# Holding seven in-place weight differences in program order, inside block 2's first product

## The chip, the cores and the metric

The kernel runs on one core of a Trainium2 chip. The metric is device time in microseconds, from one launch that has the inputs in the chip's memory to the finished output there; lower is better. A profiled execution also gives a span, which runs from the first to the last instruction, and is a little shorter than the device time.

The core has engines that run side by side, each with a queue of its own that is worked off in order: TensorE (PE in the profile; PEld is its weight load), VectorE (DVE), ScalarE (ACT), GpSimd (POOL) and SyncE (SP), which here only issues transfers. SBUF is the working memory of 128 partitions, PSUM the memory into which TensorE writes its sums.

## The reference

A retention layer, step by step in time, and then a feed-forward block with a sigmoid-gated activation:

```
B, H, S, D = 4, 8, 768, 64            # q, k, v
state = zeros(B, H, D, D)
for t in range(S):
    state = gamma[h] * state + outer(k[t], v[t])
    y[t]  = (q[t] @ state) / sqrt(D)
x = y as (B*S, H*D) = (3072, 512)
h = x @ w_in                          # 512 x 2048
g = h * sigmoid(1.702 * h)
out = g @ w_out                       # 2048 x 512 -> (3072, 512), float32
```

## The kernel before, in words

The 3072 tokens are worked off in six blocks (`m` = 0 to 5). For each block the first product makes h = x · w_in with the activation behind it, and the second makes g · w_out. The steps of the retention for the next block (L287 to L310 on TensorE, with transposes L251, masks L316 and outputs L345 on VectorE) are strewn between the pieces of a second product.

**Products with fewer multiplications.** The 2 x 2 scheme with seven products instead of eight (Strassen's in Winograd's form) is used for blocks of matrices. It needs sums and differences of quarters of both operands. `sums_w1`, `sums_w2`, `sums_x` (L437 to L441, on POOL) and `sums_g` (L452 to L456) make these. After them `W2` holds seven 128-partition slots of w_out's sums, each of 8 x 256 values per partition.

From block 2 on the second product is cut twice (`down49`, seven times seven products): each of the seven slots of `W2` is itself split into four quarters b11, b12, b21, b22, and three inner sums t1, t2, t4 and one difference t3 of these are wanted. They don't all fit in SBUF. `inner_w2(i)` makes three of them in a scratch part of `X` with three chained VectorE subtractions (L520) and stores them to memory (`W2D`, L521; the first four stores are issued by SP, the last three by POOL). Each call has to wait until the store of the call before has landed, since all use the same scratch. The calls stand at seven places of blocks 0 and 1, the list `INNER`; the last three are in block 1, behind its pieces 12, 15 and 18. Later a ring in SBUF is filled from `W2D` again (`stream`, L543).

**The seven differences of the title.** The fourth inner value, t3 = b22 - b12, replaces b12 in place: `inner_w2_t3(i)`, one VectorE subtraction of 128 x 512 values on line 527, called for i = 0 to 6. It needs b12 in its old state no more: the call of `inner_w2(i)` has read it, and block 1, which uses the slots of W2 uncut, must have done its products with that slot. In the program these calls stand in the loop over the rounds d = 0 to 3 of block 2's first product `up(d)`, two behind each of the first three rounds and one behind the last.

**A round of the first product** (`up`, L463 to L505) has seven matrix products of TensorE, 8 matmul instructions each, in the order x, y1, x, y2, x, y3, x. The four to `x` add up in one PSUM tile, and between them ScalarE copies what has been summed (p1 on L477, u on L484, vv on L491). VectorE adds these copies to y1, y2 and y3 (L480, L488, L494, L496), ScalarE applies the activation (L391, within `hidden`), and VectorE ends the round with four differences of the result (L502 to L505). TensorE can't add to x before the copy of it has been read. The copies p1 and t share one buffer (tag s1), and so does the `t` of block 1's second product. Behind round 0 come the two transposes L251 of a retention step.

**The end of block 1.** `down(1)` has 28 pieces. Its last additions to the output (L683) are made on VectorE into `o`, which has two buffers, and each is stored by a transfer that POOL issues (L684). Four POOL subtractions prepare the activations (L460), POOL makes the decayed keys (L272), and then `sums_x` on POOL prepares X for block 2 (L438 to L441).

**What sets the order.** TensorE's queue has the order of the program. The other queues are ordered ahead of time by a planner, which works with estimates of its own for the time of each instruction: of the instructions that could go next it takes an early one, and may draw an instruction ahead of others that stand before it in the program. `tc.keep_in_program_order(...)` binds an instruction behind the one that was written before it on the same engine, as an order only and not as a wait for its end. L520, L521, L251, L316, L345, L454 to L456, L460 and L684 are held so. L480, L505, L683, L272 and L438 to L441 aren't, and nor is L527.

Of the kernel before, what the change touches and what calls it, by code (L numbers as in the profile page):

```python
# [28 lines left out]
def kernel(  # L29
# [29 lines left out]
    pe, act, dve, pool, sp = nc.tensor, nc.scalar, nc.vector, nc.gpsimd, nc.sync  # L59
# [450 lines left out]
    def w2q(w):  # L510

        return [W2[:, w, u::2, e * P:(e + 1) * P] for u in range(2) for e in range(2)]
# [11 lines left out]
    def inner_w2_t3(i):  # L524

        b11, b12, b21, b22 = w2q(ORDER[i][1])
        dve.tensor_sub(b12, b22, b12)  # L527

    def sums_g_outer(k):

# [334 lines left out]
    for m in range(NB):  # L865
# [13 lines left out]
        if m > 1:  # L879
            if m > 2:  # L880
                W1B[:] = [late.tile([P, 2, 7, 2, P], F32, name=f"W1B{i}", tag=f"late{i}") for i in range(2)]
                pool.dma_start(W1B[0], W1D[0])
            for d in range(NP // 2):
                up(d)
                if d == 0 and m > 2:
                    pool.dma_start(W1B[1], W1D[1])
                if d == 0 and m < NB - 1:
                    turn((m + 1) * CB + 1)
                if d == NP // 2 - 2:
                    ring = begin_ring()  # L890
                if m == 2 and d < 2:
                    tc.keep_in_program_order(sp.dma_start(W1D[d], W1B[d]))
                if m == 2:
                    for i in range(2 * d, min(7, 2 * d + 2)):
                        inner_w2_t3(i)
# [62 lines left out]
```

## Time and profile before

| | |
|---|---|
| median of 6 runs | 673.8 us |
| lowest and highest | 671.99 and 676.49 us |
| the profiled execution | 671.99 us |
| its span | 670.3 us |
| granted clock of TensorE | 0.996 |
| block 1's last pieces end, block 2's first product begins | 267.16 us |
| block 2's second product begins | 319.64 us |

Times within the profile are microseconds from the start of the span. In the timeline each line has the start, the duration (for several instructions in one line, of all of them), the engine, the line of the code, the operation and its tiles, output before the arrow and inputs behind it. A bracket tells how long the engine was idle before and what ended the idle time. In the list of waits a line gives the waiting engine and line, what it waited for, the total, the count and the longest.

### The profile page before, as it was taken

What the parts mean: (1) busy time and instruction counts of PE and PEld (TensorE: products, weight loads), DVE (VectorE), ACT (ScalarE), POOL (GpSimd) and SP (SyncE); (2) the same over time, 40 slices, a digit from 0 to 9 for tenths busy, and PEclk for the clock granted to TensorE, in tenths of its full rate; (3) what the DMA queues carried; (4) which work ended last, traced back from release to release, by engine and by line L of the source; (5) the groups of instructions that cost most, each with busy time, mean ns of one, the idle gap of its engine ahead of it and who ended that gap; (6) DMA issues with size and microseconds to landing.
All of it is one profiled execution on the core that took longest, in us unless ns stands there. A gap on an engine that the chain in (4) does not pass through costs nothing.

```text
span 670.3 us, 15330 instructions
## 1 busy us (share of the span) xinstructions
PE 653.1 (97%) x6502; PEld 567.0 (85%) x6502; DVE 439.3 (66%) x614; ACT 156.9 (23%) x313; POOL 171.6 (26%) x192
## 2 busy tenths in 40 slices
PE   6899999999999999799999999999999999999997
PEld 4788864747888888688999988999988999988997
DVE  4798880879845879454986264996264995254965
ACT  5675523321000000233110233110233110233110
POOL 3000000020278325200345700254800255400000
PEclk9899999999999999999999999999999999999999
DMA  9999742332303546354286652277662243602142
GB/s 184 220 218 232 190 126 80 133 89 46 71 13 130 166 107 162 87 169 177 68 197 161 195 154 95 65 175 175 171 190 94 64 145 111 249 2 95 50 156 96
DMA packets 143781, 88.98 MB, mean 133 GB/s; under 512 B 129472, under 2 KB 130752, under 8 KB 142688
## 3 DMA queue, kind: packets, MB, share of 16 engines
q1 hardware_dynamic: 134224, 45.97, 30.4%
q0 software_dynamic: 7184, 40.78, 16.9%
q10 hardware_dynamic: 2304, 1.25, 0.6%
q8 instruction: 51, 0.84, 0.5%
q14 instruction: 18, 0.15, 0.1%
HBM read 72.37 MB, written 15.47 MB: 131 GB/s over the span
## 4 chain that ended last, share of the span: by engine, by line
PE 90%; DMA 3%; DVE 2%; SPq 2%; POOL 1%; issue 1%; ACT 0%; POOLq 0%; ACTq 0%; DVEq 0%
PE pq L574 26%; PE px L470 16%; PE py L470 12%; PE pd L707 10%; PE ph L412 8%; PE ph L425 8%; PE pt L248 2%; PE pa L287 2%; PE py L310 2%; PE pa L295 1%; PE py L304 1%; DMA kn_in<-in_k_dram 1%; DMA q_in<-in_q_dram 1%; SPq L137 1%; DMA W2D<-X 1%
## 5 line engine op out<-in xcount | busy, mean ns | idle before, releaser
L574 PE MATMUL pq<-W,G 128*128 128x128 f32 x672 | 80.2, 276 | 0.0
L574 PEld LDWEIGHTS pq<-W,G 128*128 128x128 f32 x672 | 77.6, 192 | 0.6
L543 POOL DMA_DIRECT2D ring<-W2D x28 | 15.4, 551 | 230.8 <-PE px L470 120.4
L470 PE MATMUL px<-X,W1A 128*128 128x256 f32 x256 | 60.0, 380 | 3.0 <-ACT p L477 3.0
L470 PE MATMUL px<-X,W1B 128*128 128x256 f32 x256 | 59.8, 379 | 0.0
L574 PE MATMUL pq<-ring,own 128*128 128x128 f32 x448 | 59.8, 276 | 0.0
L470 PEld LDWEIGHTS px<-X,W1A 128*128 128x128 f32 x256 | 48.2, 190 | 9.9 <-issue 3.3
L574 PEld LDWEIGHTS pq<-ring,own 128*128 128x128 f32 x448 | 54.5, 192 | 0.4
L470 PEld LDWEIGHTS px<-X,W1B 128*128 128x128 f32 x256 | 48.6, 190 | 6.6
L707 PE MATMUL pd<-W,G 128*128 128x256 f32 x224 | 49.8, 381 | 0.1
L707 PEld LDWEIGHTS pd<-W,G 128*128 128x128 f32 x224 | 42.1, 190 | 6.3 <-POOL G L460 0.5
L470 PE MATMUL py<-X,W1A 128*128 128x256 f32 x192 | 45.5, 380 | 0.6 <-DVE o L683 0.6
L470 PE MATMUL py<-X,W1B 128*128 128x256 f32 x192 | 45.4, 379 | 0.0
L391 ACT ACTIVATE G<-G 128x512 f32<-128x512 f32 x48 | 30.2, 630 | 51.1 <-DVE G L480 32.4
L470 PEld LDWEIGHTS py<-X,W1A 128*128 128x128 f32 x192 | 36.4, 190 | 5.9 <-DVE o L683 1.0
L470 PEld LDWEIGHTS py<-X,W1B 128*128 128x128 f32 x192 | 36.5, 190 | 5.0
L488 DVE TENSOR_TENSOR t<-py,u 128x512 f32<-128x512 f32 x16 | 11.1, 692 | 35.7 <-PE py L470 35.7
L477 ACT ACTIVATE p<-px 128x512 f32<-128x512 f32 x16 | 9.6, 597 | 100.4 <-PE px L470 87.4
L574 PE MATMUL pq<-ring,G 128*128 128x128 f32 x224 | 29.6, 275 | 0.0
L574 PE MATMUL pq<-W,own 128*128 128x128 f32 x224 | 29.6, 275 | 0.0
L412 PE MATMUL ph<-X,W1A 128*128 128x256 f32 x128 | 29.1, 383 | 0.2 <-DVE X L345 0.2
L502 DVE TENSOR_TENSOR G<-G 128x512 f32<-128x512 f32 (+2 forms) x24 | 12.3, 513 | 25.7 <-ACT G L391 25.7
(203 smaller groups left out, 1181.5 us busy)
## 6 DMA issues: line engine op xcount, KB each, us to landing
ring<-W2D POOLq DMA_DIRECT2D x28, 768.0 KB, 4.9
W1B<-W1D POOLq DMA_DIRECT2D x6, 1792.0 KB, 9.2
W<-in_moe_w_in_dram SPq DMA_DIRECT2D x12, 512.0 KB, 5.2
W<-in_moe_w_out_dram SPq DMA_DIRECT2D x10, 512.0 KB, 3.7
out_dram<-o POOLq DMA_DIRECT2D x20, 256.0 KB, 3.2
v_in<-in_v_dram SPq DMA_DIRECT2D x64, 64.0 KB, 3.2
q_sq<-in_q_dram SPq DMA_DIRECT2D x128, 32.0 KB, 2.2
k_sq<-in_k_dram SPq DMA_DIRECT2D x128, 32.0 KB, 2.2
```

Of the source, the lines that this page charges most:

```text
L248: pe.matmul(p[n][HALF[r], s, :], x[n][:, HP * r + s, :], ident, start=True, stop=True)
L287: pe.matmul(pa[HALF[w], u, 0, s, :], kt[HALF[u], w, s, :], qt[HALF[u], w, s, :], start=True, stop=True)
L310: pe.matmul(py[HALF[o], w, 0, 2 * u + s2 if f < 2 * CB else 2 * s2 + u, :], vn[HALF[w], HP * u + s, :], a[HALF[w], u, s, :], start=True, s ...
L391: pin(act.activation(g, h[:, i], AF.Gelu_apprx_sigmoid))
L412: pe.matmul(h[:, ab], w, X[:, 2 * th + c // 2, c % 2, :], start=(ab == 0 and c == 0), stop=(c == 3), skip_group_check=True)
L425: pe.matmul(h, w, X1[:, c // 2:4:2, c % 2, :], start=(c == 0), stop=(c == 3))
L470: pe.matmul(acc[:, u, :], t[:, q1 + u, sa, c, :], X[:, sb, c, :], start=(start and u == 0 and c == 0), stop=(stop and c == 1), skip_group_ ...
L488: dve.tensor_add(tt, z, u)
L502: dve.tensor_sub(q[0][1], q[0][0], q[0][1])
L543: pool.dma_start(c, W2D[i])
L574: pe.matmul(p0[:, j, :], a[:, d], w[:, d], start=(new and j == 0 and d == 0), stop=(d == NP // 2 - 1), skip_group_check=True)
L707: pe.matmul(p0[:, n, :], g1(m, p, sa)[:, n * P:(n + 1) * P], W2[:, sb, p, :], start=(new and p == 0 and n == 0), stop=(last and p == NP - ...
```

## The change

The subtraction of `inner_w2_t3` is bound behind what was written before it on VectorE. The first of the two behind a round is so bound behind the round's last VectorE instruction (behind round 0 these are the transposes), and the second behind the first.

```diff
     def inner_w2_t3(i):
 
         b11, b12, b21, b22 = w2q(ORDER[i][1])
-        dve.tensor_sub(b12, b22, b12)
+        tc.keep_in_program_order(dve.tensor_sub(b12, b22, b12))
```

The calls, which stay where they are:

```
        for d in range(NP // 2):
            up(d)
            ...
            if m == 2:
                for i in range(2 * d, min(7, 2 * d + 2)):
                    inner_w2_t3(i)
```

## The prediction

> **What bounds the kernel now.** I read the page first, then TensorE's waits from 258 to 330 us, then the timeline of all engines from 255 to 276 us, then VectorE, ScalarE and TensorE through block 2's first product (267 to 320 us).
>
> ```profile
> PE 653.1 (97%) x6502; PEld 567.0 (85%) x6502; DVE 439.3 (66%) x614; ACT 156.9 (23%) x313; POOL 171.6 (26%) x192
> ```
>
> TensorE is busy 97% of the 670.3 us span, so only its gaps can be won, and whatever makes a gap is lost in full. Its waits between 258 and 330 us are two, both on the seam from block 1 to block 2:
>
> ```profile
> PE px L470 <- ACT p L477: 3.0, 1, 3.0
> PE py L470 <- DVE o L683: 0.6, 1, 0.6
> ```
>
> The seven differences are L527. The answer for that line gives shortest, median and longest in ns and the first and last start:
>
> ```profile
> L527 DVE TENSOR_TENSOR W<-W x7: 674/681/7976, 217.3 to 270.1; 128x512 f32<-128x512 f32 x7
> ```
>
> So all seven now run in block 1 and the seam, six of them at 0.7 to 1.8 us, and one takes 7.98 us. The timeline of the seam shows which (start, duration, engine, line; in brackets the idle time before it and what ended it):
>
> ```profile
> 256.07 0.69 DVE L520 TENSOR_TENSOR X<-W,X 128x512 f32<-128x512 f32 x1
> 256.68 0.68 DVE L527 TENSOR_TENSOR W<-W 128x512 f32<-128x512 f32 x1
> 257.28 0.68 DVE L520 TENSOR_TENSOR X<-W,X 128x512 f32<-128x512 f32 x1
> ...
> 258.26 0.53 POOL L521 DMA_DIRECT2D W2D<-X  x1 [6.83 <-DVE X L520]
> ...
> 258.81 4.95 POOL L460 TENSOR_TENSOR G<-G 128x512 f32<-128x512 f32 x4
> ...
> 261.01 7.98 DVE L527 TENSOR_TENSOR W<-W 128x512 f32<-128x512 f32 x1
> ...
> 268.51 1.60 POOL L441 TENSOR_TENSOR X<-X 128x512 f32<-128x512 f32 x1
> 268.91 1.27 DVE L683 TENSOR_TENSOR o<-pd,vv 128x512 f32<-128x512 f32 x2
> ...
> 270.05 1.51 POOL L684 DMA_DIRECT2D out_dram<-o  x2
> ...
> 273.05 0.69 DVE L683 TENSOR_TENSOR o<-pd,t 128x512 f32<-128x512 f32 x1 [2.27 <-DMA out_dram<-o]
> 273.85 0.60 ACT L477 ACTIVATE p<-px 128x512 f32<-128x512 f32 x1 [13.06 <-DVE o L683]
> ...
> 274.59 1.75 PE L470 MATMUL px<-X,W1A 128*128 128x256 f32 x7 [2.96 <-ACT p L477]
> ```
>
> The 3.0 us wait hangs on a chain through POOL, not on the 7.98 us difference itself. POOL works without a pause from 258.26: the store L521, four L460, L272, L438 to L441, then two stores L684. The third L683 needs an `o` buffer, free only when the first L684 has landed (270.05 + 2.87 in the chain of waits, + 0.13 = 273.05); L477 writes the slot (tag s1) that this L683 reads; and TensorE can't go on in px before L477 has read it. The L684 are pinned behind L441, so they can't start before the sums of X are done, however early VectorE is.
>
> **What the change removes.** Seven subtractions leave block 1. Each is worth only what it does to that chain.
>
> The one at 227.56 stands in a stretch in which VectorE has no idle time, from 223.85 to 244.1; its successor starts 0.60 later. The stretch ends in the L520 of the fifth inner sum (241.40), whose store L521 at 244.08 must land (4.34 us) before the next L520 can write X; so again to the last L520s at 255.35. Whether every step moves up: the twelve L454 to L456 behind it wait for TensorE's products, but the last product they need ends about 1 us before they start. Gain 0.60, bounds 0 and 0.68.
>
> The one at 256.68 stands between two dependent L520: 1.21 us apart, where the pair at 242.10 takes 1.42 for two, 0.72 apart. Gain 0.49, bounds 0 and 0.60.
>
> The one at 261.01 competes with POOL. VectorE instructions that take one input from PSUM aren't held (L316, L328, L345 take 0.68, 0.68 and 0.69 while L460 runs), so the two L683 would end by about 262.5. That takes away TensorE's 0.6 us wait, but TensorE then only meets the 3.0 us wait earlier. What counts is L441: it took 1.60 us where the shortest of its four runs is 1.256 and the median 1.268, and it began 0.08 after L440's end (268.43), where the other sums follow without a gap. That is the moment the held difference got through. Gain 0.33 + 0.08 = 0.4, bounds 0 and 0.42.
>
> The other four end in VectorE waits (for W2D's landing, or for `o`) and are worth nothing; the one at 217.32 is also beside POOL's L434, 1.71 instead of 1.27, and POOL idles 0.93 soon after.
>
> Sum: 0.60 + 0.49 + 0.4 = 1.5 us (lowest 0, highest all of TensorE's gaps at the seam, 3.0 + 0.6 = 3.6). What is late next is the same chain: px goes on at 273.1 instead of 274.59, while TensorE has been free since about 270.4; about 2.7 us of the idle time stays. L272 in it needs a landing of kn at 259.79 and would start at 262.6, so this doesn't bind.
>
> The Trainium skill, "SBUF — State Buffer", section "Who interferes with whom", says that a VectorE instruction with two SBUF inputs and a GpSimd instruction that reads SBUF exclude each other, the later one waiting until the first is done. The trace agrees that there is exclusion, but not on its length: 7.98 us is past eight ends of POOL instructions. By the page the difference would have got through at the first of them, near 261.3, L441 would not have been touched, and the sum would be 1.1 instead of 1.5; the measured rows decide.
>
> **What it adds.** Two differences each behind rounds 1, 2 and 3 of block 2's first product and one behind round 4, on VectorE's queue, 0.60 apart when unhindered (256.68 to 257.28). No DMA, no new data to wait for: block 1 is done with W2. POOL is idle from 274.8 to 308.0, so holding as at 261.01 is excluded in rounds 1 and 2. Behind them queues the next round's L480, whose result ScalarE's L391 takes; and L484, which TensorE needs, queues behind L391 on ScalarE:
>
> ```profile
> 287.74 0.67 DVE L251 STREAM_TRANSPOSE kT<-k_sq 128x512 f32<-128x512 f32 x1
> 288.33 0.65 DVE L480 TENSOR_TENSOR G<-py,p 128x512 f32<-128x512 f32 x1
> ...
> 289.01 0.63 ACT L391 ACTIVATE G<-G 128x512 f32<-128x512 f32 x1 [3.13 <-DVE G L480]
> 289.55 0.58 ACT L484 ACTIVATE u<-px 128x512 f32<-128x512 f32 x1
> ...
> 290.21 1.97 PE L470 MATMUL px<-X,W1A 128*128 128x256 f32 x8
> ```
>
> Behind round 1 there is no slack: L484 ends at 290.13 and the product starts at 290.21, already 0.08 late by its length of 1.97 against 1.89. Two differences ahead of L480 put L480 at 289.53 to 290.22, L391 at 290.26, L484 at 290.80 to 291.38, and the product at 291.5: 1.3 us lost, if ScalarE's order stays. But its order and VectorE's are set by a planner with estimates of its own, free to put L484 first, whose px is ready at about 288.7, once L480 is planned 1.2 us later; or to put L480 ahead. So 0 to 1.3; I take 0, since the planner now has the two only about half a microsecond apart.
>
> Behind rounds 2 and 3 there are no transposes. L480 moves from 299.22 to 300.33, L391 ends at 301.69, L484 at 302.18; with the 0.13 us from L477's end to px at the seam that is 302.31 against a product at 302.37. Round 3 likewise 314.40 against 314.46. Cover of 0.06 us: 0, bounds 0 and 0.3 each (0.72 instead of 0.60 per difference). The one behind round 4 comes before the own sums L564 and L565, which end 0.6 later, at 323.67 and 324.29; their products start at 324.10 and 325.00. Nothing lost.
>
> **The sum against the times.** The profiled execution took 671.99 us, 1.7 beyond its span, and was the fastest of six; 671.99 - 1.5 = 670.5. The median is 673.8, 1.8 above. Had the held difference got through only after L441 (269.67), L684 would have started at about 271.14 (0.56 to its end, 0.61 for L683 behind it, 0.30 to the store), 1.1 later than in this execution. So of the 1.8 between 0 and 1.1 may be this hold, which the change ends; that gives 671.2 to 672.3. I take 671.6.
>
> **The rivals.** What a measurement here can tell from no change is about 0.3%, 2.0 us: below 671.8 is faster, above 675.8 slower.
>
> A. Forecast, 0.60: the chain moves up by 1.5, rounds stay whole: 671.6, its own range 670.5 to 672.5. It straddles the bound: faster in about six parts of ten.
>
> B. The queue of round 1 keeps L391 ahead of L484: 1.5 - 1.3 leaves 0.2: 672.9, no change. For it: that order in all rounds of blocks 2 and 3. Against it: the planner sees the later L480. 0.15.
>
> C. More than the chain: the hold is worse in ordinary executions, or the stores land sooner, and most of 3.6 goes: 670.2 or less. 0.12.
>
> D. Slower: the differences go ahead of L480 in rounds 1, 2 and 3 at more than 0.60. At 0.72 it is 1.5 + 0.3 + 0.3 = 2.1; at 1.75, as the one at 217.32 took beside POOL, 3.6 + 2.2 + 2.2 = 8. It decides once three rounds lose over 3.5 us against the 1.5 gained, about 1.0 us for each difference; or over 2.0 if the chain doesn't move. Against it: POOL's silence until 308. With the price between, 677. 0.10.
>
> E. Nothing moves, since the chain's steps were bound by landings: 673.8. 0.03.
>
> **How the numbers follow.** Faster: 0.6 of A (0.36) and C's most, 0.10: 0.46. Slower: D 0.10, and 0.03 for other queues that the planner sets anew: 0.13. The rest, 0.41, is within 0.3%. The range leaves out D and the ends: 669.6 (C at 4.2) to 673.9 (B with its rounds 2 and 3, and E).
>
> **What would show it.** L527 seven times at 0.68, from about 287 to 322; no VectorE instruction of 8 us; L441 at 1.27; the last store L521 at 257.2; px's wait on L477 about 2.7 and the one on L683 gone; L484 of round 2 ahead of L391, or a new wait of px on L484 of 1.3 (then B). Wrong, if L684 starts no earlier, or if the wait on L477 shrinks by over 2.

## The result, and the profile after

The changed kernel takes 671.87 us (median of 37 runs, 668.86 to 674.86), the kernel before 673.4 us (median of 79 runs). The ratio is 0.9973, 95% interval [0.9963, 0.9983]: 0.27% or 1.8 us faster by the ratio (the two medians are 1.5 us apart), clear of the measurement's interval and just inside the 0.3% that the prediction counted as no change. Forecast were 671.6 us and a range of 669.6 to 673.9.

The profiled execution after is not one of the quicker ones: its span is 670.9 us, 0.6 longer than the span of the profile before. So spans can't be subtracted here; the profile has to be read by stage. The page's engine line, and TensorE's waits (total, count, longest):

```profile
PE 653.4 (97%) x6502; PEld 567.7 (85%) x6502; DVE 431.1 (64%) x614; ACT 157.0 (23%) x313; POOL 170.7 (25%) x192
```

```profile
PE px L470 <- ACT p L477: 2.2, 1, 2.2
```

VectorE's busy time fell by 8.2 us, of which 7.3 is the one long difference; none of that is time won by itself. TensorE's wait on L477 is 2.2 us and the wait of py on L683 is gone. The answer for line 527 shows all seven differences in block 2, at ordinary length:

```profile
L527 DVE TENSOR_TENSOR W<-W x7: 647/683/685, 289.4 to 323.5; 128x512 f32<-128x512 f32 x7
```

The seam in the timeline after, beside the prediction's lines:

```profile
257.94 0.53 POOL L521 DMA_DIRECT2D W2D<-X  x1 [5.83 <-DVE X L520]
...
262.22 1.29 DVE L683 TENSOR_TENSOR o<-pd,vv 128x512 f32<-128x512 f32 x2 [2.05 <-ACT vv L679]
...
268.20 1.27 POOL L441 TENSOR_TENSOR X<-X 128x512 f32<-128x512 f32 x1
...
269.41 1.51 POOL L684 DMA_DIRECT2D out_dram<-o  x2
...
272.54 0.69 DVE L683 TENSOR_TENSOR o<-pd,t 128x512 f32<-128x512 f32 x1 [9.04 <-DMA out_dram<-o]
...
273.35 0.60 ACT L477 ACTIVATE p<-px 128x512 f32<-128x512 f32 x1 [11.17 <-DVE o L683]
...
274.09 3.33 PE L470 MATMUL px<-X,W1A 128*128 128x256 f32 x7 [2.24 <-ACT p L477]
```

The two L683 on vv are done 5.9 us before POOL comes to their stores: the chain still goes through POOL, L684, its landing, the last L683 and L477. To compare profiles, everything is measured from L287 of block 1's last step to the start of block 2's second px ("the measure" below). Before:

```profile
254.81 0.69 PE L287 MATMUL pa<-qT,kT 64*64 64x64 f32 x32
```

After:

```profile
256.21 0.69 PE L287 MATMUL pa<-qT,kT 64*64 64x64 f32 x32
```

Before it is 274.59 - 254.81 = 19.78 us, after it is 274.09 - 256.21 = 17.88: 1.90 won. The way from the start of the span to this L287 says nothing of the change: it is 254.5 to 257.6 us over all profiles, with either order.

The last line of the seam shows what nobody had counted. The second px has eight matmul instructions that take 1.80 us to the next product in the profile before; here seven of them take 3.33. The stretches of the timeline by engine tell why (busy time and count for PE, PEld, DVE, ACT, POOL, then TensorE's granted clock, the DMA share and GB/s):

```profile
268.20:274.10 5.90, 3.66 (x18) 2.90 (x17) 0.76 (x2) 0.60 (x1) 3.28 (x4) 1.00 0.66 163
274.10:277.60 3.50, 3.50 (x9) 2.84 (x10) 0.63 (x1) 0.63 (x1) 0.16 (x1) 0.51 0.63 161
277.60:282.80 5.20, 5.20 (x26) 4.58 (x25) 1.39 (x2) 1.35 (x3) 0.00 (x0) 1.00 0.01 1
```

Behind the idle time the granted clock is 0.51 for 3.5 us and then 1.00 again. The next py starts at 277.58, 3.49 us behind px instead of 1.80. That costs 1.7 us, nearly all of what the earlier chain had won in this execution. The longer span comes of this and of an L287 that is 1.40 us later.

Block 2's first product behind that, from the second py to the first pq, takes 320.74 - 277.58 = 43.16 us; before it was 319.64 - 276.39 = 43.25. The differences cost TensorE nothing there. VectorE, ScalarE and TensorE behind round 1, from the timeline after:

```profile
289.38 1.25 DVE L527 TENSOR_TENSOR W<-W 128x512 f32<-128x512 f32 x2
290.55 0.68 DVE L480 TENSOR_TENSOR G<-py,p 128x512 f32<-128x512 f32 x1
...
289.92 0.60 ACT L484 ACTIVATE u<-px 128x512 f32<-128x512 f32 x1 [2.86 <-PE px L470]
291.27 0.63 ACT L391 ACTIVATE G<-G 128x512 f32<-128x512 f32 x1 [0.74 <-DVE G L480]
...
291.39 1.89 PE L470 MATMUL px<-X,W1A 128*128 128x256 f32 x8
```

L480 has gone behind both differences, and the planner has put L484 ahead of L391, at this place alone. It is done at 290.52, 0.87 us before its product starts.

### The profile page after: what moved, and what is told of

Its sections match the earlier page's. It is cut to its first block, busy times and chain, and to the rows that moved or that the text cites. A ratio compares the mean times of both kernels' runs of the same rounds, so it can differ in the third digit from the quotient of the medians.

```text
span 670.9 us, 15330 instructions
## 1 busy us (share of the span) xinstructions
PE 653.4 (97%) x6502; PEld 567.7 (85%) x6502; DVE 431.1 (64%) x614; ACT 157.0 (23%) x313; POOL 170.7 (25%) x192
## 3 DMA queue, kind: packets, MB, share of 16 engines
HBM read 72.37 MB, written 15.47 MB: 131 GB/s over the span
## 4 chain that ended last, share of the span: by engine, by line
PE 89%; DMA 5%; DVE 3%; POOL 1%; issue 1%; ACT 1%; SPq 0%; POOLq 0%; ACTq 0%; DVEq 0%
PE pq L574 26%; PE px L470 17%; PE py L470 12%; PE pd L707 10%; PE ph L425 8%; PE ph L412 8%; DMA kn_in<-in_k_dram 2%; PE pa L287 2%; PE pt L248 2%; PE pa L295 2%; PE py L310 2%; PE py L304 1%; DMA W2D<-X 1%; DMA v_in<-in_v_dram 1%; DVE X L520 1%
## 5 line engine op out<-in xcount | busy, mean ns | idle before, releaser
L470 PE MATMUL px<-X,W1A 128*128 128x256 f32 x256 | 61.6, 387 | 2.2 <-ACT p L477 2.2
L391 ACT ACTIVATE G<-G 128x512 f32<-128x512 f32 x48 | 30.2, 630 | 50.9 <-DVE G L480 32.3
L477 ACT ACTIVATE p<-px 128x512 f32<-128x512 f32 x16 | 9.6, 597 | 98.0 <-PE px L470 86.8
```

Source lines behind the costliest of these rows:

```text
L391: pin(act.activation(g, h[:, i], AF.Gelu_apprx_sigmoid))
L470: pe.matmul(acc[:, u, :], t[:, q1 + u, sa, c, :], X[:, sb, c, :], start=(start and u == 0 and c == 0), stop=(stop and c == 1), skip_group_ ...
```

## The experiments

In the code cuts `rounds[0]` counts the calls of `up`, so that 1 is block 2's first round.

The theory: the seam's wait is set by a chain that runs from the stores of the inner sums through POOL's queue to L684, its landing, the last L683 and L477; the change wins by starting this chain earlier. The rivals: the long difference beside POOL was itself the loss; or the wait has another cause.

**Half of the change: the long difference alone.** Each difference can be left floating or held:

```diff
-        dve.tensor_sub(b12, b22, b12)
+        (tc.keep_in_program_order if i in (2, 3) else (lambda x: x))(dve.tensor_sub(b12, b22, b12))
```

> Only the differences i = 2 and 3 are held, those that ran at 243.44 and, with 7.98 us, at 261.01. Measure: from the L287 of block 1's last step to the second px of block 2 (19.78 us before, 17.88 after the change). Chain theory: VectorE's hold is gone and so is py's wait on L683, but the chain through POOL starts as late as before; only L441 falls from 1.60 to 1.27: 19.45 us, a median 0.3 us lower, ratio 0.9995. Rival, that the 7.98 us hold itself made the loss: 17.9 to 18.3 us and the whole gain, ratio 0.9973.

Ratio 1.0 [0.9984, 1.0017], and 20.40 us on the measure. Taking away the 7.98 us brought nothing, so it was not the loss. But L441 did not fall to 1.27 as expected, since the next difference came to the same place, and the measure is 0.6 us above the kernel before instead of 0.3 below: the last store L521 came 3.83 us behind L287 instead of 3.45, and L684 took 3.22 us to land instead of 3.00. Its timeline:

```profile
269.67 2.49 DVE L527 TENSOR_TENSOR W<-W 128x512 f32<-128x512 f32 x1 [4.21 <-PE pd L707]
...
271.68 1.60 POOL L441 TENSOR_TENSOR X<-X 128x512 f32<-128x512 f32 x1
...
278.00 2.72 PE L470 MATMUL px<-X,W1A 128*128 128x256 f32 x8 [4.05 <-ACT p L477]
```

**The other half: the ones in the way of the inner sums.** The same edit with `i in (0, 1, 6)`.

> Only the differences i = 0, 1 and 6 are held, those that ran at 217.32, 227.56 and 256.68; the one with 7.98 us stays beside POOL. Chain theory: the last store L521 is issued 1.1 us earlier (0.60 + 0.49), more if the landings before it are shorter as in the profile after; the measure from L287 to the second px is 18.3 to 18.7 us, a long L527 and py's wait on L683 stay; a median lower by 1.1 to 1.6 us, ratio 0.9976 to 0.9984. Rival, that the hold made the loss: 19.8 us, no change.

Ratio 0.9975 [0.9958, 0.9991], 275.48 - 257.15 = 18.33 us on the measure, with the long difference still in place. Py's wait on L683, which was expected to stay, is gone, since the difference, as long as before, now ends 12.66 us behind L287 instead of 14.18:

```profile
259.09 0.53 POOL L521 DMA_DIRECT2D W2D<-X  x1 [5.96 <-DVE X L520]
...
261.83 7.98 DVE L527 TENSOR_TENSOR W<-W 128x512 f32<-128x512 f32 x1
...
275.48 3.65 PE L470 MATMUL px<-X,W1A 128*128 128x256 f32 x8 [2.69 <-ACT p L477]
```

The last L521 comes 1.94 us behind the L287, where it was 3.45 before and is 1.73 in the changed kernel. Holding three differences that each took at most 1.75 us brings the gain; the one of 7.98 us carries none of it that could be measured.

**Cutting the chain at its end: another buffer for the first p1**, in the changed kernel.

```diff
-        p1 = one.tile([P, 2, TH], F32, name="p1", tag="s1")
+        p1 = one.tile([P, 2, TH], F32, name="p1", tag="s3" if rounds[0] == 1 else "s1")
```

> The changed kernel, with the first round's copy p1 in the buffer of tag s3 and not in s1, which block 1's t holds until the last L683. Chain theory: L477 needs no L683 of t any more and follows the first px; px goes on at once, about 15.5 us after the last step's L287 instead of 17.88, with at most 0.3 us of wait on L484 later in the round, since L480 stands behind that L683 on VectorE. No idle time of TensorE, so no stretch at half clock there either: 2.2 us below the changed kernel, and up to 3.5 where that has the slow stretch; ratio to before 0.992 to 0.995. Rival: something else is late with it (X from L441, or the weights), and a wait of 2 us stays: ratio 0.997.

Ratio 0.9914 [0.9889, 0.9939]; the measure is 269.99 - 254.51 = 15.48 us, and no wait on L477 is left:

```profile
268.51 0.60 ACT L477 ACTIVATE p<-px 128x512 f32<-128x512 f32 x1 [8.03 <-PE px L470]
...
269.99 1.89 PE L470 MATMUL px<-X,W1A 128*128 128x256 f32 x8
...
271.05 0.69 DVE L683 TENSOR_TENSOR o<-pd,t 128x512 f32<-128x512 f32 x1 [9.24 <-DMA out_dram<-o]
```

The last L683 waits for its landing as before, but now behind the second px.

**Cutting it in the middle: the two stores from ScalarE's queue**, in the changed kernel.

```diff
-            tc.keep_in_program_order((pool if m < NB - 1 else act).dma_start(rows[th, e], o))
+            tc.keep_in_program_order((pool if m < NB - 1 and (m, th) != (1, 1) else act).dma_start(rows[th, e], o))
```

> The changed kernel, with the two stores of the L683 on vv issued by ScalarE instead of by POOL behind the sums of X. Chain theory: the stores go out at about 262 and 263 us, land by 266.5, the last L683 waits only for its product and ends at about 269, and L477 follows the first px at once: px's wait falls from 2.24 to under 0.5 us, the measure to 15.5 to 16.0 us; ratio to before 0.992 to 0.995. Rival, that the store's place on POOL does not matter, since ScalarE's queue or the landing is as late: wait 2 us, ratio 0.997.

Ratio 0.9917 [0.9896, 0.9939], 271.71 - 256.24 = 15.47 us. The stores went out at 264.63 and not at 262, but the landing was still early enough: the last L683 now waits for its product.

```profile
264.63 1.01 ACTq L684 DMA_DIRECT2D out_dram<-o  x2
...
268.46 0.69 DVE L683 TENSOR_TENSOR o<-pd,t 128x512 f32<-128x512 f32 x1 [4.93 <-PE pd L707]
```

**Both cuts together**, in the changed kernel.

> The changed kernel with both remedies, p1 of the first round in s3 and the two stores issued by ScalarE. Either took the whole wait on L477 away, so there is nothing left for the second: 15.5 us from L287 to the second px, no wait on L484, ratio to before 0.991 to 0.993, the same as with one.

Ratio 0.9918 [0.9896, 0.9939], 270.88 - 255.40 = 15.48 us: the second cut finds nothing left. One of them is enough. The three ratios lie 3.7 to 4.0 us below the changed kernel's, a little lower than was expected of either cut alone, while the measure fell by 2.4. The intervals allow for 2.4; a slow stretch that goes with the wait would add to it, but how much isn't shown.

**The first cut without the change**: the kernel before with p1 in s3.

> The kernel before, differences not held, with the first round's copy p1 in the buffer of tag s3. Chain theory: the wait of px on L477 (2.96 us in the profile before) goes nearly away, since L477 now needs the two L683 on vv only. What the long difference costs by itself is then seen: L683 ends at about 270.2, py waits 0.6 us, and L480, behind the L683 on t, makes L484 late and px wait another 0.7 to 0.9 us. From the last step's L287 to the second px 16.2 to 16.6 us (19.78 before, 15.48 with the change and p1 in s3); ratio to before 0.993 to 0.995, so within 1.5 us of the changed kernel with the same buffer. Rival, that the difference held beside POOL is the main loss: 18 us or more, ratio 0.997 to 1.0.

Ratio 0.9934 [0.992, 0.9947], 273.30 - 256.97 = 16.33 us, a long L527 of 7.97 us, py's wait on L683 of 0.57 and a wait of px on L484 of 0.45 later, less than the 0.7 to 0.9 expected. This is the long difference's price where the chain doesn't hide it. By the starts of the products it is more than the two waits together: the measure is 16.33 - 15.48 = 0.85 above the same kernel with the change, and the third px comes another 0.52 later, 4.07 us behind the second instead of 3.55: 1.4 us. The ratios of the two (0.9934 and 0.9914) have overlapping intervals, so in the time this remainder isn't shown.

**The price of case B**: the changed kernel with ScalarE's old order behind round 1.

```diff
-        act.activation(u, x, AF.Copy)
+        (tc.keep_in_program_order if rounds[0] == 2 else (lambda x: x))(act.activation(u, x, AF.Copy))
```

> The changed kernel, with L484 of block 2's second round bound behind L391 on ScalarE, the order of the kernel before. By the prediction's price for case B: L480 stands behind two differences, L391 behind L480, L484 behind L391, and the third px of that round waits 1.3 us on L484; everything else as in the changed kernel, so 1.3 us above it, ratio to before 0.999. Rival: L391 and L484 are ready early enough, no wait over 0.2 us, ratio 0.997.

The wait came as named, but smaller:

```profile
290.27 0.63 ACT L391 ACTIVATE G<-G 128x512 f32<-128x512 f32 x1 [4.20 <-DVE G L480]
...
290.81 0.58 ACT L484 ACTIVATE u<-px 128x512 f32<-128x512 f32 x1
...
291.44 1.99 PE L470 MATMUL px<-X,W1A 128*128 128x256 f32 x8 [0.88 <-ACT u L484]
```

The px starts 291.44 - 288.67 = 2.77 us behind its py instead of 1.73: 1.04 us lost, not 1.3. The time doesn't show it: 0.9973 [0.9959, 0.9987] is the changed kernel's own ratio, and the two intervals, about 0.9 and 0.7 us each way, can't tell 1.0 us from none.

**Filling the idle time.** To part the idle time from the clock, matmuls whose results are used nowhere were put where TensorE waits, two in the changed kernel and three in the one before. `fill(n)` makes n of them, 128 x 512, from the identity:

```diff
-        product(y, 1, 1, True, True)
+        product(y, 1, 1, True, True); rounds[0] == 1 and fill(2)
```

> The changed kernel with two further matmuls of 128 x 512 whose results are used nowhere, put behind the first py of block 2, where TensorE otherwise idles 2.24 us. They do not shorten the chain: the second px starts 17.9 us after the last step's L287 as without them. Theory that the idle time itself lowers the clock: the second px then runs at full clock, 1.8 us and not 3.5, in the profile, and the median falls by up to 1.7 us against the changed kernel, by 0.8 if half of its executions have the slow stretch: ratio to before 0.995 to 0.9965. Rival, that the clock falls for another reason: px 3.5 us in some profiles still, ratio 0.997.

> The kernel before with three further matmuls of 128 x 512, results used nowhere, behind the first py of block 2, where TensorE idles some 3 us. Theory of two parts: the change wins by an earlier chain (about 1.9 us here) and, apart from that, both kernels lose up to 1.7 us to a slow clock behind the idle time in some executions. Then the second px starts 19.8 us after the last step's L287 as before, runs at full clock, and the ratio to before is 0.9975 to 0.999; the changed kernel with its two further matmuls (0.9935) stays about 2 us below. Rival, that the change wins only because it shortens the idle time and so the clock: ratio 0.994 like that kernel.

The changed kernel with filling:

```profile
273.58 1.97 PE L470 MATMUL px<-X,W1A 128*128 128x256 f32 x8 [0.41 <-ACT p L477]
275.38 1.89 PE L470 MATMUL py<-X,W1A 128*128 128x256 f32 x8
```

The kernel before with filling:

```profile
274.30 1.97 PE L470 MATMUL px<-X,W1A 128*128 128x256 f32 x8
276.10 1.89 PE L470 MATMUL py<-X,W1A 128*128 128x256 f32 x8
```

In the changed kernel the ratio is 0.9935 [0.9921, 0.9949] and the measure 273.58 - 255.81 = 17.77 us, as without filling, with the second px at full clock, 1.80 us to the next product. In the kernel before the ratio is 0.9977 [0.9962, 0.9993] and the measure 274.30 - 255.94 = 18.36 us, px also at 1.80. So both gain by filling alone, about 2.6 and 1.5 us, though it shortens nothing in the chain; and with both filled, the changed kernel remains lower, in intervals that don't meet. The change does win apart from what filling wins, though the 2.8 us between the two are more than the chain's 1.4, which no run here explains.

That the gain by filling is the clock's is supported for one of the two only. Each execution has its mean granted clock on record, and its span times what the clock lacks of 1 is an estimate of the time lost to it. In the kernel before this falls with filling from 3.4 us (16 executions of the same session) to 1.7 (12 executions), about the gain. In the changed kernel it is 3.1 us without filling (37 executions) and 3.1 with it (5 executions): the 2.6 us, more than the 1.7 expected, are not accounted for. The estimate is rough, as it takes in another slow stretch far ahead of the seam (0.50 from 22 to 24 us in the profile after), which differs from execution to execution.

The 18.36 is lower than expected (19.8), with the differences in their old places: the last L521 came 2.00 us behind L287 and not 3.45. Two landings were shorter by 0.77 together, and L287 itself came 0.55 later against VectorE's queue. The start of the chain moves by more than a microsecond from one execution to another.

**Both kernels again, for a second profile.**

> The changed kernel once more, for a second profile of it. Chain theory: 17.4 to 18.4 us from the last step's L287 to the second px, by how soon the stores to W2D land; L441 at 1.27; L527 seven times at 0.68. The second px takes 1.8 us or, with a slow clock, up to 3.5.

> The kernel before once more, for a second profile. The prediction's step from the profiled execution to the median held that the long L527 ends later in ordinary executions, up to behind L441, and starts L684 up to 1.1 us later. By that theory its duration varies from 8 to 9.3 us; by the rival it is 7.97 us again, as in the two experiments that kept it, and the measure from L287 to the second px varies only with the landings, 19.5 to 20.5 us.

After: 273.44 - 256.04 = 17.40 us, L441 at 1.27 and the second px at 1.81. Before: 276.49 - 256.92 = 19.57; L527, and the timeline of the seam:

```profile
L527 DVE TENSOR_TENSOR W<-W x7: 674/682/7977, 219.4 to 271.9; 128x512 f32<-128x512 f32 x7
```

```profile
276.49 3.75 PE L470 MATMUL px<-X,W1A 128*128 128x256 f32 x8 [3.03 <-ACT p L477]
...
280.04 3.10 PE L470 MATMUL py<-X,W1A 128*128 128x256 f32 x8
...
282.97 1.89 PE L470 MATMUL px<-X,W1A 128*128 128x256 f32 x8
```

Here the slow clock takes in px and py: 282.97 - 276.49 = 6.48 us for two products that take 1.80 + 1.73 at full clock, 2.95 lost in an execution of 676.15 us.

## Why the prediction was right, and where it was not

**The chain** was forecast at 1.5 us and measured at 1.90 between the two profiles shown. Over all profiles whose chain was left whole, the kernel before has 19.78, 19.57 and, with filling, 18.36 us (mean 19.2), the changed one 17.88, 17.40, 17.77 and, up to there the same, 18.14 (mean 17.8): 1.4. L684 starts 15.24 us behind L287 before and 13.20 after, so the sign that would have proved the chain wrong, an L684 no earlier, did not appear. By its terms:

- The difference at 227.56, forecast 0.60. On VectorE's own queue, from the L345 ahead of it to the first L520 of the fifth inner sum, it is 241.40 - 226.95 = 14.45 us before and 242.05 - 228.32 = 13.73 after. Over all profiles it is 14.32 to 14.45 in the five that have the difference there and 13.72 to 13.87 in the eight that don't: 0.6.

```profile
226.95 0.69 DVE L345 TENSOR_TENSOR X<-py,tmp 128x512 f32<-128x512 f32 x1
...
241.40 0.67 DVE L520 TENSOR_TENSOR X<-W 128x512 f32<-128x512 f32 x1
```

```profile
228.32 0.69 DVE L345 TENSOR_TENSOR X<-py,tmp 128x512 f32<-128x512 f32 x1
...
242.05 0.67 DVE L520 TENSOR_TENSOR X<-W 128x512 f32<-128x512 f32 x1
```

- The one between two L520, forecast 0.49: from the last inner sum's first L520 to its store L521 it is 2.44 us instead of 2.91, 0.47. It is 2.43 or 2.44 in all profiles without the difference there and 2.91 or 2.92 in all others.
- L441, forecast 0.33 + 0.08: it took 1.27 instead of 1.60, which is the 0.33. It is 1.26 or 1.27 in all profiles where no difference is held beside it and 1.60 or 1.61 in all others. The 0.08 was wrong: L441 begins 1.34 us behind L440 after as before. POOL pauses there whatever VectorE does; this pause let the held difference through.
- Not foreseen, in the two profiles shown: the last landing before L520 took 3.94 us instead of 4.46 (0.52 won), the first store L684 3.13 instead of 3.00 to the last L683 (0.13 lost). These are no merit of the change: that landing takes 3.85 to 4.52 us in the profiles that have the difference at 227.56 held, 3.89 to 4.46 in the others.

**The cost in the rounds** was forecast at 0, and is 0, for the reason given: the planner put L484 ahead of L391 where that mattered. Case B's price was 1.04 instead of 1.3; part of that is that the two differences delayed L480 by only 1.17 us and the transposes ahead of them began 0.12 sooner behind L505. Rounds 2 and 3 kept their order and their cover sufficed.

**What is late next**: a wait of about 2.7 us on L477 was forecast, 2.24, 1.76 and 2.49 were measured; the two cuts show that it is the forecast chain and nothing else. The 2.7 was also wrongly worked out. With py 1.73 us behind px, and 1.89 long, TensorE is free at 270.8 and not at 270.4, so that 2.3 would have stayed.

**The step that failed** is the one from the profiled execution to the median. The prediction put up to 1.1 of the 1.8 us between them to the long difference, which would end behind L441 in ordinary executions. It doesn't: it took 7.98, 7.98, 7.97, 7.98 and 7.98 us in the five profiles that have it, always let through in the same pause. What the prediction lacked is the clock behind the wait. In 7 profiles TensorE waits 1.76 to 4.05 us for L477; in 4 of these the products behind run slowly and lose 1.7 to 3.0 us (waits of 2.24, 2.69, 3.03 and 4.05), in 3 they don't (1.76, 2.49 and, in the first profile before, 2.96). In the 6 where fillings or cuts leave waits under 0.6 us, none does. The profile before happened to be free of it and the profile after was not.

So it is partly luck that 671.6 came near 671.87. The 1.5 from the chain stands, but the 0.7 beyond it was given a false reason, and the forecast started from 673.8, the median of six runs, where 79 runs have 673.4. How large a share of the change's 1.8 us the clock has is not settled, as only profiles show where a slow stretch lies. An estimate from the mean granted clocks, as above, has 3.8 us lost before (the 56 executions on record with their clock) and 3.1 after (37): about 0.6 us may be the clock's, with the stretch at 20 us in it.

**Two rules beside the runs.** The Trainium skill, "SBUF — State Buffer", section "Who interferes with whom", has the later instruction wait until the first is done; five times the difference was held past six ends of POOL instructions (the prediction counted eight: behind 261.01 end three L460, L272, L438 and L439) and got through only in a pause of 0.08 us behind the seventh, L440. The Trainium skill, "TensorE: Matmul & The Clock Gate", section "What's actually happening", has the clock halved after an idle window of about 3.4 us that runs free of the kernel. The half clock (0.51) and the variation from execution to execution agree; the length of the wait doesn't: 2.24 us, less than one such window, was enough in the profile after.

## What to carry to other kernels

A long bar on a side engine need not be the loss: here the 7.98 us instruction cost nothing measurable, as long as another chain ended later, while short ones delayed a store that the next stage waited for, and only following the wait back to its start told them apart. Where one wait is left, cutting its chain (another buffer, or another queue for one store: ratio 0.9914 to 0.9918 against 0.9973 for the change) is worth more than starting it earlier. Of the six profiles here with a TensorE wait of 2.24 us or more, four lost another 1.7 to 3.0 us to a slow clock behind it, so price such a wait with that, and don't compare kernels by one profile's span.

## What the runs showed of the hardware

- TensorE's granted clock fell to 0.51 for 3.5 us behind a wait of 2.24 us, and not behind one of 2.96 us in another execution. With two or three matmuls without use in the gap the clock stayed at full there in the one profile of each kernel, and the time was lower by 2.6 us (change) and about 1.5 us (before), though they shortened nothing in the chain.
- A VectorE instruction with two inputs in SBUF was held beside POOL's instructions across six of their ends, 7.97 to 7.98 us each time, and got through at a pause of 0.08 us, lengthening the next POOL instruction from 1.27 to 1.60 us. VectorE instructions with an input in PSUM ran at 0.68 us beside the same POOL instructions.
